# Windowed attention and a squared-ReLU MLP: one list plan for all engines from the second chunk on, second products spread between the seven, weights streamed in seven pieces

## The chip, the core and the metric

The kernel runs on one core of a Trainium2 chip. The metric is the device time of one execution in microseconds (us). Five instruction queues work beside each other, each in its own fixed order: PE (matrix products), DVE and ACT (element-wise work and reading of PSUM, the accumulation banks), POOL (element-wise work on SBUF) and SP (issues nearly all DMA transfers). An instruction waits on semaphores for what it reads, and everything behind it on its own queue waits with it.

## The reference

```python
q, k, v: (8, 8, 576, 64)  w_in: (512, 2048)  w_out: (2048, 512)
scores = q @ k.T / 8 - slope[h] * |i - j|       # keys with 0 <= i - j < 128 only
attn   = softmax(scores)
x      = concat over heads of attn @ v          # (4608, 512)
out    = relu(x @ w_in) ** 2 @ w_out            # (4608, 512)
```

## The kernel before

The 4608 tokens are cut into nine **chunks** of 512, the 2048 hidden units into 16 blocks f of 128. Numbers are split into a high and a low part, so every product takes three matmuls (high by high, high by low, low by high).

In chunks 0 and 1 a block of hidden units is a **first product** of 12 matmuls (line 222); its bank is read by the Relu on ACT (line 232), then squared on DVE and split again into `hh` and `hl`. From chunk 2 on two blocks are made together, as **pair** n = 8c + j, by **the seven** (lines 295 to 345): seven products M1 to M7 of six half-width matmuls each, in the manner of Strassen, on sums of weights and sums of inputs. Three pieces of PSUM hold them: `chain`, through which M1, M6, M7 and M4 accumulate, and two halves of `rest`. Between the products these pieces must be read (**drained**) into `four`: M6 waits until ACT has copied `chain` after M1 (line 315), M2 until DVE has copied `rest` (319), M7 for line 322, M3 and M4 for the additions of line 312. The **second product** of a block f (line 359) is four **parts** of three matmuls, one for each 128 output columns.

The sums of weights are made once, in chunk 1, by `weight_sums` (lines 243 to 271: six additions on POOL, a split on ACT and DVE, per pair j) and kept in DRAM. `stream` (273) brings them back for each pair in two DMA transfers, of 1024 and 768 KB.

Attention runs ahead of the MLP. A **couple** q is one chunk and one pair of heads, in two **segments** s = 0, 1. A **visit** on PE, after every fourth first product and later after every second pair, does three things: it multiplies couple q - 1's probabilities with its values, half of them (line 702), makes couple q's scores (709), and finishes the values. For each segment of couple q then follows its **probability chain**: copy (594, 601) on ACT, masking (613, 617) on DVE, minimum (381) on DVE and exponential (388) on ACT four times, sums (395, 396), scaling (400) on POOL, a block transposition (452) on DVE, four DMA writes of 64 KB to DRAM (456), one read of 256 KB back in another order (461), and two selections on POOL (465). The next visit needs both segments' selections. The values of couple q - 1 are split on ACT, DVE and POOL (`tee`, `tees`, lines 666 to 691); for head pairs p = 2 and 3 they also give the sums of inputs, and with p = 3 the next chunk is complete.

What sets the order: `Plan` (line 793) is a list scheduler; steps have an engine, a duration, predecessors, a due time and rooms (buffers) that they take and free, and it emits step by step what could start first, the earliest due among those. Before, only `start` (847), chunk 0 with the attention ahead of it, is planned by it. From chunk 1 on (lines 991 to 1023) PE's order is as written, and the other engines' order is made by the framework's own scheduler from its timing model, steered by priorities (`high_priority`) and one dependency (`soft`, after the Relu or the first drain).

## Time and profile before

| what | us |
|---|---|
| runs shown: 1006.80, 1003.14, 1007.87; median | 1006.80 |
| profiled execution, its own time | 1004.76 |
| its span, first to last instruction | 1003.1 |
| PE busy | 936.0 |
| DVE / ACT / POOL busy | 602.3 / 435.1 / 290.8 |
| first product of chunk 1 starts | 141.4 |
| first of the seven (chunk 2) starts | 269.2 |
| last chunk's own pairs (no visits) start | 908.9 |

Busy shares are means over stages with different limits; what bounds a stage is read from who waits for whom in it. A busy PE is not PE at its full rate: the granted clock stands in a row of its own.

### The profile page before, as it was taken

The page shows a single profiled execution, that of the slowest core. Times are in us where ns is not written, and L with a number is a line of the kernel's source. Part 1 is how long each engine was busy: PE and PEld are TensorE (multiplying, and loading weights), DVE is VectorE, ACT ScalarE, POOL GpSimd, SP SyncE. Part 2 cuts the span into 40 slices and gives each one's busy share as a digit, 9 for nine tenths or more (in the row PEclk, how much of TensorE's full clock was granted, in tenths as well). Part 3 has the DMA queues.
Part 4 walks back from the last instruction along what each step waited for, and adds up shares of the span by engine and source line. Part 5 has one row for each costly group of instructions (what it writes and reads, how often), then busy time and mean ns, then how long its engine had stood idle before and what let it go on. Part 6 is the DMA issues. An engine that isn't in the chain of part 4 may idle for free.

```text
span 1003.1 us, 22438 instructions
## 1 busy us (share of the span) xinstructions
PE 936.0 (93%) x8496; PEld 817.7 (82%) x8500; DVE 602.3 (60%) x1622; ACT 435.1 (43%) x1241; POOL 290.8 (29%) x362
## 2 busy tenths in 40 slices
PE   9898999978789989999999989999999989999998
PEld 5687887757679878898888878888898878988997
DVE  6987855465545565566666656666565574665333
ACT  7897644344434434334434434343343433443222
POOL 4112335785622222222322232223222322221000
PEclk9999999998989999999999999999999999999999
DMA  9986633457476666676666657767766675555541
GB/s 350 404 315 210 196 82 142 121 189 247 133 264 227 225 205 200 230 231 225 213 218 229 228 180 256 227 226 226 266 225 214 214 224 178 199 183 213 182 147 43
DMA packets 95819, 212.89 MB, mean 212 GB/s; under 512 B 10464, under 2 KB 44384, under 8 KB 88544
## 3 DMA queue, kind: packets, MB, share of 16 engines
q1 hardware_dynamic: 95280, 210.81, 63.2%
q8 instruction: 67, 1.10, 0.4%
q10 hardware_dynamic: 432, 0.66, 0.2%
q14 instruction: 40, 0.33, 0.1%
HBM read 170.52 MB, written 40.89 MB: 211 GB/s over the span
## 4 chain that ended last, share of the span: by engine, by line
PE 52%; DMA 17%; DVE 12%; POOL 8%; ACT 6%; issue 3%; SPq 1%; POOLq 0%; DVEq 0%; ACTq 0%
PE acc L359 22%; PE chain L309 10%; PE rest L309 8%; DMA pp<-way 5%; PE g L222 4%; POOL pp L465 4%; DMA way<-pp 3%; DMA flow<-ws 3%; PE s L702 3%; DVE t L381 3%; DVE t L613 3%; DMA raw<-in_dram 2%; PE g L709 2%; ACT t L601 2%; ACT t L388 2%
## 5 line engine op out<-in xcount | busy, mean ns | idle before, releaser
L359 PE MATMUL acc<-hh,w 128*128 128x512 f32 x1152 | 411.1, 399 | 0.0
L359 PEld LDWEIGHTS acc<-hh,w 128*128 128x128 f32 x1152 | 226.6, 197 | 39.0 <-issue 5.6
L359 PE MATMUL acc<-hl,w 128*128 128x512 f32 x576 | 227.1, 394 | 0.0
L465 POOL TENSOR_SCALAR_AFFINE_SELECT pp<-pp 128x512 f32<-128x512 f32 x128 | 104.0, 820 | 306.3 <-DMA pp<-way 196.0
L309 PEld LDWEIGHTS rest<-xu,flow 128*128 128x128 f32 x1008 | 147.6, 198 | 24.0 <-DVE four L319 10.0
L309 PE MATMUL chain<-tees,flow 128*128 128x256 f32 x1008 | 152.4, 287 | 13.6 <-ACT four L315 12.3
L309 PE MATMUL rest<-xu,flow 128*128 128x256 f32 x1008 | 150.7, 286 | 9.3 <-DVE four L319 5.6
L309 PEld LDWEIGHTS chain<-tees,flow 128*128 128x128 f32 x1008 | 134.7, 199 | 18.1 <-ACT four L315 15.6
L359 PEld LDWEIGHTS acc<-hl,w 128*128 128x128 f32 x576 | 113.2, 197 | 12.0
L312 DVE TENSOR_TENSOR four<-four,rest 128x256 f32<-128x256 f32 x112 | 46.9, 419 | 111.6 <-PE rest L309 111.0
L336 ACT COPY four<-chain 128x256 f32<-128x256 f32 x56 | 20.9, 373 | 211.8 <-PE chain L309 211.8
L388 ACT ACTIVATE t<-t,nm 128x128 f32<-128x128 f32 x256 | 100.4, 394 | 26.0 <-DVE nm L381 25.7
L222 PE MATMUL g<-xu,w 128*128 128x512 f32 x384 | 98.9, 407 | 11.2 <-ACT r L232 11.2
L400 POOL TENSOR_TENSOR t<-t,nm 128x512 f32<-128x512 f32 x64 | 68.0, 1066 | 142.5 <-DVE nm L396 139.5
L222 PEld LDWEIGHTS g<-xu,w 128*128 128x128 f32 x384 | 78.0, 214 | 26.7 <-ACT r L232 13.3
L343 DVE SCALAR_TENSOR_TENSOR four<-four 128x512 f32<-128x512 f32 x112 | 81.7, 766 | 2.5 <-ACT four L336 0.4
L345 DVE TENSOR_TENSOR hl<-four,hh 128x512 fp32r<-128x512 f32 x112 | 77.2, 718 | 6.7
L702 PE MATMUL s<-pp,v 64*64 64x64 f32 (+1 forms) x1792 | 61.1, 261 | 21.1 <-POOL pp L465 21.0
L344 ACT CAST hh<-four 128x512 fp32r<-128x512 f32 x112 | 68.8, 620 | 23.0 <-DVE four L343 22.6
L319 DVE COPY four<-rest 128x256 f32<-128x256 f32 x56 | 23.4, 418 | 87.1 <-PE rest L309 86.8
L702 PEld LDWEIGHTS s<-pp,v 64*64 64x64 f32 x1792 | 46.6, 141 | 33.7 <-POOL pp L465 27.3
L452 DVE STREAM_TRANSPOSE pp<-t 128x512 f32<-128x512 f32 x64 | 44.8, 706 | 34.7 <-POOL t L400 32.7
(102 smaller groups left out, 1102.7 us busy)
## 6 DMA issues: line engine op xcount, KB each, us to landing
flow<-ws SPq DMA_DIRECT2D x56, 1024.0 KB, 5.4
flow<-ws SPq DMA_DIRECT2D x56, 768.0 KB, 5.3
raw<-in_dram SPq DMA_DIRECT2D x32, 512.0 KB, 8.7
way<-pp SPq DMA_DIRECT2D x256, 64.0 KB, 3.2
pp<-way SPq DMA_DIRECT2D x64, 256.0 KB, 3.7
qk<-in_dram SPq DMA_DIRECT2D x32, 320.0 KB, 3.9
v<-in_dram SPq DMA_DIRECT2D x32, 320.0 KB, 4.4
qk<-in_dram SPq DMA_DIRECT2D x38, 256.0 KB, 4.6
```

The source lines that it names most:

```text
L222: nc.tensor.matmul(g, w, xs[cc][:, part], start=i == 0, stop=i == 11)
L309: nc.tensor.matmul(to, w, x, start=start and k == 0, stop=k == 5, skip_group_check=True)
L312: add = lambda to, x: nc.vector.tensor_tensor(to, to, x, op=ALU.add)
L343: nc.vector.scalar_tensor_tensor(r, r, 0.0, r, op0=ALU.max, op1=ALU.mult)
L344: nc.scalar.copy(hh, r)
L345: nc.vector.tensor_tensor(hl, r, hh.bitcast(F32), op=ALU.subtract)
L359: nc.tensor.matmul(self.acc[m], w, h, start=(f == 0 and i == 0), stop=(f == NF - 1 and i == 2))
L388: return self.nc.scalar.activation(self.t[:, m], self.t[:, m], AF.Exp, bias=nm[:, 4 + m : 5 + m], scale=-1.0, accum_out=nm[:, m : m + 1],)
L400: self.nc.gpsimd.tensor_tensor(*(x.rearrange("p (j i) c -> p j i c", j=2) for x in (self.t, self.t)), self.rec.unsqueeze(3).to_broadcast([ ...
L452: nc.vector.transpose(squares.rearrange("p b m c -> p m b c"), self.t.rearrange("p m (b c) -> p m b c", c=32))
L465: nc.gpsimd.affine_select(to, self.own, pattern=[[-32 * sign, 4], [0, 4], [-sign, 32]], compare_op=op, fill=0.0, base=0, channel_multiplie ...
L702: made.append(mm(to, w, x, start=first and n < 2, stop=not first, skip_group_check=True))
```

## The change

From chunk 1 on `middle` lists every step of every engine for a second `Plan`, with durations and due times, and the plan emits them; the framework's scheduler orders nothing any more. PE's order is still as listed, as each PE step has the one before as predecessor. Within it:

- **Second products** lag one part further and stand two by two between the seven: M1, two parts, M5 M6, two, M2 M7, two (one in even pairs), M3 M4, two (three after a visit). Before it was one part in each of the first three gaps and five behind M4.
- **Visits** stand right behind M4 of odd pairs; before one more part lay between.
- **Weights** come in seven transfers of 256 KB into seven rooms; each is issued for pair n + 2 once the product of pair n that read its room is done. For odd pairs they also wait for the plan's step that reads back the probabilities of a certain earlier visit.
- **`weight_sums`** becomes single steps, one pair j behind every second first product; before two pairs j were issued behind each visit. Its ACT and DVE steps and the transfers of its results are halved.
- The squares go to rooms of their own (`r`, `spare`), so that `four` is free earlier; memsets of masked columns become steps of their own (`fill`); copying out (`give`) and sending (`send`) too.
- The values' split becomes eleven (or six) steps. They are due late, but for p = 3, where the next chunk needs them.

```diff
+    def stream(self, n, i):
+        self.nc.sync.dma_start(self.flow[n % 2][i].bitcast(F32), self.sums[n % 8][:, i])
...
+    def squared(self, n, f):
...
+        x, r = self.four[f], self.spare if f else self.hp.tile([128, 512], F32, name="r", bufs=1)
+        nc.vector.scalar_tensor_tensor(r, x, 0.0, x, op0=ALU.max, op1=ALU.mult)
...
-    def __init__(self):
-        self.steps, self.count = {}, {}
+    def __init__(self, wait=WAIT, port=PORT):
+        self.steps, self.count, self.wait, self.port = {}, {}, wait, port
...
+DRAINS = {
+    "s1": (ACT, 0.32, "M1"), "R": (DVE, 0.4, "M5"), "s2": (ACT, 0.32, "M6"), "C11": (DVE, 0.4, "M2"),
+    "C22": (DVE, 0.4, "M7"), "C12": (DVE, 0.4, "M3"), "C21": (ACT, 0.32, "M4"),
+}
+BEHIND = {"M6": ("s1",), "M2": ("R",), "M7": ("s2",), "M3": ("C11",), "M4": ("C22",)}
...
+def middle(K, waiting):
+    P = Plan(0.7, ("t", "ws"))
...
+    def chain(q, s, V):
...
+        d = V + (7.5 if s else 5.5)
+        for m in range(4):
+            P.add(n("t", m), DVE, 0.22, (n("t", m - 1) if m else n("fold"),), V + 1.8 + 1.4 * s, do(G.top, m))
+            P.add(n("e", m), ACT, 0.4, (n("t", m),) + ((n("e", m - 1),) if m else ()), V + 2 + 1.5 * s, do(G.exp, m))
+        P.add(n("sum"), DVE, 0.42, (n("e", 3),), d + 2.2, G.sums)
+        P.add(n("norm"), POOL, 1.15, (n("sum"),), d + 2.7, G.norm)
+        turned(q, s, d + 4, (n("norm"),))
+
+    def turned(q, s, d, after):
...
+        P.add(n("square"), DVE, 0.72, after, d, step, "pp", "t")
+        P.add(n("write"), "SP", 1.8, (n("square"),), d + 1, step)
+        P.add(n("read"), "SP", 1.4, (n("write"),), d + 4.9, step)
+        P.add(n("before"), POOL, 0.81, (n("read"),), d + 8.2, step)
+        P.add(n("same"), POOL, 0.81, (n("before"),), d + 9, step)
...
+    def stream(n, i, t):
+        gate = 2 * ((2 * n - 7 - FIRST) // 4 + 9) + 1
+        if n < FULL:
+            after = [(PIECES[i], n - 2)] if (PIECES[i], n - 2) in P.steps else []
...
+            if n % 2 and ("read", gate) in P.steps:
+                after.append(("read", gate))
+            P.add(("flow", n, i), "SP", 0.8, tuple(after), t + 17, do(K.stream, n, i))
...
+        counts = (2, 2, 2, 3 if n % 2 else 2) if n % 2 or n >= FULL - 8 else (2, 2, 1, 2)
...
+            if names[0] == "M3" and V:
+                visit((2 * n + 1 - FIRST) // 4 + 9)
+            second(count)
```

Three places in the order, before and after. **First, POOL in chunk 1**, ahead of its third visit. `both` are sums of weights, `pp` the probabilities that the visit waits for (line 465 before, 484 now). Before:

```order
L258 TENSOR_TENSOR both4_2523<-w7_606 128x512
L465 AFFINE_SELECT pp_2220<-pp_2220 128x512
L267 TENSOR_TENSOR both2_2230<-both2_2230 128x256
L258 TENSOR_TENSOR both4_2523<-w7_606 128x512
L465 AFFINE_SELECT pp_2220<-pp_2220 128x512
L264 TENSOR_TENSOR both4_2523<-both4_2523 128x256
L465 AFFINE_SELECT pp_2303<-pp_2303 128x512
L266 TENSOR_TENSOR both4_2523<-both4_2523 128x256
L265 TENSOR_TENSOR both4_2523<-both4_2523 128x256
L465 AFFINE_SELECT pp_2303<-pp_2303 128x512
```

POOL after, at the same visit:

```order
L261 TENSOR_TENSOR both4_2038<-w7_606 128x512 x2
L268 TENSOR_TENSOR both4_2038<-both4_2038 128x256
L270 TENSOR_TENSOR both4_2038<-both4_2038 128x256
L484 AFFINE_SELECT pp_2358<-pp_2358 128x512 x2
L484 AFFINE_SELECT pp_2366<-pp_2366 128x512 x2
L272 TENSOR_TENSOR both4_2038<-both4_2038 128x256
L274 TENSOR_TENSOR both4_2038<-both4_2038 128x256
```

The four selections now stand together; before five weight sums lay between them.

**Second, PE and ACT at pair 28**, the first pair behind a visit. On PE `acc` are second products, `chain` and `rest` the seven. PE before:

```order
L309 MATMUL chain_4907<-xu_3513,flow4_1694 128x256 x3
L359 MATMUL acc_4372<-hh_4763,w8_677 128x512
L359 MATMUL acc_4372<-hl_4764,w8_677 128x512
L359 MATMUL acc_4372<-hh_4763,w8_677 128x512
L309 MATMUL rest_4908<-xu_3178,flow4_1694 128x256 x3
L309 MATMUL rest_4908<-xu_3513,flow4_1694 128x256 x3
L309 MATMUL chain_4907<-tees12_1685,flow4_1694 128x256 x6
```

PE after, from the same product M1 to the same product M6:

```order
L319 MATMUL chain_4941<-xu_3639,flow4_0_1673 128x256 x3
L376 MATMUL acc_4473<-hh_4745,w6_576 128x512
L376 MATMUL acc_4473<-hl_4746,w6_576 128x512
L376 MATMUL acc_4473<-hh_4745,w6_576 128x512
L376 MATMUL acc_4438<-hh_4847,w8_677 128x512
L376 MATMUL acc_4438<-hl_4848,w8_677 128x512
L376 MATMUL acc_4438<-hh_4847,w8_677 128x512
L319 MATMUL rest_4967<-xu_3232,flow4_1_1674 128x256 x3
L319 MATMUL rest_4967<-xu_3639,flow4_1_1674 128x256 x3
L319 MATMUL chain_4941<-tees12_1664,flow4_2_1675 128x256 x6
```

Between M1 and M6, which needs the copy of `chain`, there are now two parts and M5, before one part and M5.

ACT there, before (601 and 594 copy the scores, 388 are exponentials, 315 is the copy that M6 waits for, 670, 671 and 674 split the values):

```order
L601 COPY t_4848<-g_4800 128x2x128
L594 COPY t_4846<-g_4800 128x512
L670 CAST xu_4859<-s_4783 128x256
L671 COPY o_4860<-s_4783 128x256
L388 ACTIVATE t_4846,nm_4847<-t_4846,nm_4847 128x128 x4
L315 COPY four_1698<-chain_4907 128x256
L388 ACTIVATE t_4848,nm_4849<-t_4848,nm_4849 128x128 x4
L674 CAST xu_4859<-o_4860 128x256
L322 COPY four_1698<-chain_4907 128x256
```

ACT after (613 and 620, 407, 327 and 331, 684 to 688 in the same roles):

```order
L613 COPY t_4385<-g_4855 128x512
L620 COPY t_4682<-g_4855 64x2x128
L620 COPY t_4682<-g_4855 128x2x128
L407 ACTIVATE t_4385,nm_4386<-t_4385,nm_4386 128x128 x4
L327 COPY four0_1687<-chain_4941 128x256
L407 ACTIVATE t_4682,nm_4683<-t_4682,nm_4683 128x128 x4
L351 CAST hh_4981<-spare_1689 128x512
L686 CAST xu_4987<-s_4827 128x256
L331 COPY four0_1687<-chain_4941 128x256
L684 COPY o_4994<-s_4827 128x256
```

One segment's copy comes first now, and the values' split has moved behind the exponentials.

**Third, SP at the same pair** (`flow` are weights, `way` the probabilities' writes to DRAM, `pp` their reads). Before:

```order
L456 DMA way_4551<-pp_4549 32x4x128 x4
L278 DMA flow4_1694<-ws4_112 128x2048
L461 DMA pp_4549<-way_4551 128x512
L456 DMA way_4600<-pp_4598 32x4x128 x4
L278 DMA flow6_1695<-ws4_112 128x1536
L461 DMA pp_4598<-way_4600 128x512
L278 DMA flow8_1696<-ws5_113 128x2048
```

SP after:

```order
L288 DMA flow4_0_1673<-ws4_112 128x512
L175 DMA v_4631<-in_1_dram 128x640
L288 DMA flow4_1_1674<-ws4_112 128x512
L288 DMA flow4_2_1675<-ws4_112 128x512
L475 DMA way_4669<-pp_4667 32x4x128 x4
L480 DMA pp_4667<-way_4669 128x512
L475 DMA way_4719<-pp_4707 32x4x128 x4
L480 DMA pp_4707<-way_4719 128x512
L288 DMA flow4_3_1676<-ws4_112 128x512
L288 DMA flow4_4_1677<-ws4_112 128x512
```

Nothing but the probabilities' own transfers stands between their first write and their last read now; before two transfers of weights lay there.

More of the change, by code (lines that the diff above doesn't have):

```diff
@@ L625, in begin, with fill @@
         self.base(s)
[L627 to L639 removed]
+    def fill(self, s):
+        self.room(s)
+        self.base(s, True)
     def values(self):
@@ L694, in visit @@
-def visit(K, old, new):
-    nc, mm = K.nc, K.nc.tensor.matmul
-    S = K.sc.tile([128, 2, 512], F32, name="s")
-    def phase(rows, first):
-        made = []
-        for n, pair in enumerate(zip(*(G.quarters(S, r) for G, r in zip(old.both, rows)))):
-            for to, w, x in pair:
-                made.append(mm(to, w, x, start=first and n < 2, stop=not first, skip_group_check=True))
-        return made
-    last = phase((0, 1), True)[-1]
-    if new:
-        new.S, new.B = S, K.big.tile([128, 2, 512], F32, name="g")
-        for extra, to, w, x in new.quarters():
-            made = mm(to, w, x, start=not extra, stop=True, skip_group_check=True)
-            last = made if extra else last
-    turn = nc.gpsimd.nop()
-    K.tc.add_manual_dep(turn.ins, last.ins.name, SYNC, reason="halves of the keys change banks")
-    for made in phase((1, 0), False)[:2]:
-        K.tc.add_manual_dep(made.ins, turn.ins.name, SYNC, reason="halves of the keys change banks")
-    if old.both[0].p == 3:
-        old.out(S)
-    if new:
-        new.front()
-    if old.both[0].p < 3:
-        old.out(S)
-    if new:
-        new.both[0].soft()
+        one, two = slice(0, 256), slice(256, 512)
@@ L843, in run @@
                 do()
+            for a in then.get(name, ()):
+                need[a] -= 1
+                if need[a] == 0:
+                    near.add(a)
+        assert len(end) == len(self.steps), sorted((set(self.steps) - set(end)), key=str)
         return end
```

531 lines of the change are left out of this document (337 added, 194 removed).

## The prediction

> **What bounds the kernel now.** The page first: of all engines PE alone is busy nearly throughout, and its clock digit is 8 in one slice of 40 and 9, the highest, in the others.
>
> ```profile
> PE 936.0 (93%) x8496; PEld 817.7 (82%) x8500; DVE 602.3 (60%) x1622; ACT 435.1 (43%) x1241; POOL 290.8 (29%) x362
> PEclk9999999998989999999999999999999999999999
> ```
>
> The change takes no matmul away, so the question is how far PE's stages are from running without a gap. The view of busy time by stretch, cut at the first product of chunk 1, at the first of the seven and at the last chunk's pairs (columns: stretch, its length, busy us of PE, weight loads, DVE, ACT, POOL, then clock and DMA share):
>
> ```profile
> 141.40:269.20 127.80, 108.77 (x870) 90.74 (x870) 64.38 (x135) 47.65 (x116) 82.08 (x87) 0.95 0.49 159
> 269.20:908.90 639.70, 602.96 (x6071) 540.00 (x6070) 387.88 (x1116) 257.50 (x818) 166.75 (x223) 0.98 0.68 221
> 908.90:1003.10 94.20, 90.42 (x553) 82.26 (x551) 36.85 (x68) 21.12 (x44) 1.29 (x2) 1.00 0.40 140
> ```
>
> What such a stretch takes without gaps stands in the chain that ended last (start, us), at places where PE follows PE:
>
> ```profile
> 149.93 2.76 PE acc L359 x12
> 152.69 2.76 PE g L222 x12
> ...
> 429.17 0.83 PE s L702 x32
> 431.89 3.00 PE acc L359 x12
> 453.35 0.20 PE s L702
> ...
> 947.83 3.49 PE acc L359 x15
> 958.43 3.49 PE acc L359 x15
> ```
>
> A first product takes 2.76 us, a second one 2.76, a pair in the last chunk 958.43 - 947.83 = 10.60. From one visit to the next with nothing in the way it is 453.35 - 429.17 = 24.18, of which the visit is 431.89 - 429.17 = 2.72. So **chunk 1** could take 16 x 5.52 + 4 x 2.72 = 99.2 against 127.8, and the **24 periods** of two pairs and a visit 24 x 24.18 = 580.3 against 639.7. Lost are 28.6 and 59.4, together 88.0 us. The last chunk loses nothing (8 x 10.60 and the 9.1 of the second products left over make 93.9 of its 94.2), and chunk 0 isn't touched.
>
> Who PE waited for in the two stretches (us in total, times, longest), chunk 1 in the first two rows:
>
> ```profile
> PE g L222 <- ACT r L232: 10.5, 4, 3.5
> PE s L702 <- POOL pp L465: 7.3, 2, 5.0
> ...
> PE s L702 <- POOL pp L465: 13.6, 18, 2.5
> PE chain L309 <- ACT four L315: 12.3, 13, 2.7
> PE rest L309 <- DVE four L319: 5.6, 4, 2.9
> ```
>
> Two kinds: a drain or Relu that came late, and a visit that waited for selections. The waits shown are about half of the 88 us; a good part of the rest is the clock after them. One drain wait in the timeline, what ACT did just before (chain), and the stretch behind:
>
> ```profile
> 383.12 1.26 ACT t L388 x6
> 384.38 0.27 ACT four L315
> ...
> 384.69 0.99 PE L309 MATMUL chain<-tees,flow 128*128 128x256 f32 x6 [2.44 <-ACT four L315]
> ...
> 385.70:389.10 3.40, 3.40 (x15) 3.17 (x15) 1.35 (x4) 0.74 (x5) 1.31 (x2) 0.51 0.29 61
> ```
>
> The copy that M6 needs stood behind exponentials; PE was idle for 2.44 us and then ran 3.4 us at a granted 0.51, which costs 1.7 more.
>
> **The change part by part.** *Drains and Relus (chunk 1: 10.5 and its clock; later 12.3 + 5.6 and theirs).* In the order, two parts and M5 (2 x 0.70 + 0.72 = 2.1 us) now cover the copy of `chain` where one part and M5 (1.4) did. The copy itself takes about 0.4, with at most four exponentials of about 0.4 ahead of it, and the values' split has gone behind. What would be late next is the second segment's sums on DVE, with a drain behind them. I take 0.1 per period; the bounds are 0 and today's (12.3 + 5.6) / 24 = 0.75.
>
> *POOL in chunk 1.* Ahead of its third visit the four selections stretched over 226.02 - 216.18 = 9.8 us for 4.1 of their own, with weight sums between:
>
> ```profile
> 216.18 0.96 POOL L465 TENSOR_SCALAR_AFFINE_SELECT pp<-pp 128x512 f32<-128x512 f32 x1 [0.25 <-issue]
> 218.92 0.73 POOL L465 TENSOR_SCALAR_AFFINE_SELECT pp<-pp 128x512 f32<-128x512 f32 x1
> 221.37 1.18 POOL L465 TENSOR_SCALAR_AFFINE_SELECT pp<-pp 128x512 f32<-128x512 f32 x1
> 224.81 1.21 POOL L465 TENSOR_SCALAR_AFFINE_SELECT pp<-pp 128x512 f32<-128x512 f32 x1
> ```
>
> Now they stand together. But POOL's 82.1 us stay, 83% of a stage of 99.2, with a wait for a transfer in each visit, so not all of it can go. I leave 2 us for each of the four visits and 3 for the border to chunk 2, where the seven need sums of inputs that a visit has just made: 11 of 28.6. Bounds: 5 and 28.6. Halving the splits adds eight ACT and eight DVE instructions and 16 transfers; on engines busy for 47.7 and 64.4 of the 127.8 I cost them at nothing, within these bounds.
>
> *Visits from chunk 2 on (13.6 and the clock).* The best case of before, a visit that ends at 856.45 and is followed by one at 878.03 without a wait (chain, SP's and POOL's rows):
>
> ```profile
> 856.45 3.00 PE acc L359 x12
> ...
> 863.59 1.77 SPq L456 DMA_DIRECT2D way<-pp  x4
> 867.14 2.06 SPq L456 DMA_DIRECT2D way<-pp  x4
> 869.37 0.36 SPq L461 DMA_DIRECT2D pp<-way  x1
> 873.15 0.32 SPq L461 DMA_DIRECT2D pp<-way  x1
> ...
> 876.29 1.52 POOL L465 TENSOR_SCALAR_AFFINE_SELECT pp<-pp 128x512 f32<-128x512 f32 x2 [1.09 <-DMA pp<-way]
> ...
> 878.03 0.47 PE s L702 x13
> ```
>
> First write 7.1 after the visit, last selection 21.4 after it; PE leaves 24.18 - 2.72 = 21.5. So even the best visit had no slack, and most of the window goes to transfers. Their medians from issue to landing, in chunk 1 (almost no weights on the way) and later:
>
> ```profile
> way<-pp SPq DMA_DIRECT2D x32, 64.0 KB, 2.0
> pp<-way SPq DMA_DIRECT2D x8, 256.0 KB, 2.8
> ...
> flow<-ws SPq DMA_DIRECT2D x48, 1024.0 KB, 5.5
> way<-pp SPq DMA_DIRECT2D x192, 64.0 KB, 3.7
> pp<-way SPq DMA_DIRECT2D x48, 256.0 KB, 4.1
> ```
>
> The new order has a price: SP stands at the first segment's read until its writes have landed, and the second segment's writes stand behind. From the first write on: 1.35 to the last of four issues (1.77 x 3/4), landing w, read issue 0.35, again 1.35 and w, read r, two selections 1.6, in all 4.65 + 2w + r. The first write comes about 0.5 earlier (one segment's copy, line 594, 0.6, no longer ahead), so 6.6 after the visit. With the medians of chunk 1 the selections end 6.6 + 4.65 + 4.0 + 2.8 = 18.1 after the visit, with the later ones 22.8, against 21.5: no wait, or 1.3. No weights are issued between, but a few pieces lie just ahead; I take 0.4. Every fourth visit (p = 3) makes ACT, DVE and POOL split the values first; there I take 2.0. With the drains' 0.1 per period and two half-clock stretches behind the longest of these waits (1.7 each, from the row above), 18 x 0.4 + 6 x 2.0 + 24 x 0.1 + 3.4 = 25.0 of today's 59.4 remain. Bounds: 5 and 59.4.
>
> *Weights in seven pieces.* 1792 KB per pair as before. They landed 5.5 us after the issue, with two transfers of a pair often on the way together, and a product's room is free two pairs, 21.2 us, before its next use. For odd pairs the reads of a visit, some 4 us later, come first; the cover that is left is 21.2 - 4 - 5.5, about 11 us. Issues on SP take 0.32 to 0.45 each (rows above: 1.77 for four): five more per pair, 2.3 us of 10.6, on a queue that mostly waits. I take 0; bounds 0 and, were all of it in front of the visit's writes, 2.3 per period.
>
> *The clock.* In the row above a gap of 2.44 us led to half clock, so gaps that remain near that length cost 1.7 more. The Trainium skill's "TensorE: Matmul & The Clock Gate", section "Why this matters for your kernels", wants gaps under about 3 us; by that none of my remaining gaps would cost clock, and the sum would be 3.4 us lower. The trace disagrees, with 0.51 behind 2.44 us, and the sum keeps its own.
>
> **Sum:** 1004.8 (the profiled execution, 0.2% under the median of 1006.8, so no correction) - (28.6 - 11) - (59.4 - 25.0) = 1004.8 - 17.6 - 34.4 = 952.8, say **953**.
>
> **Rivals.** *Everything hidden.* Landings as in chunk 1 and drains never late leave the lower bounds, 5 + 5: 1004.8 - 23.6 - 54.4 = 927. For it: 18.1 against 21.5. Against: p = 3 and POOL's 83%.
>
> *The visit takes the place of the drains.* Landings stay at 3.7 and 4.1: 18 x 1.3 + 6 x 3.3 = 43.2, and the six longer gaps cost 1.7 each, 10: 53 of 59.4 remain. 1004.8 - 17.6 - 6.2 = 981. For it: the window was full before; against: the weights no longer lie between.
>
> *It does not do what it says.* The plan's durations are off (its Plan gives a write and its read 3.2 on SP and 2.0 of handing over, where the rows give 1.35 + 3.7 + 4.1), each queue then stands in a wrong order and new waits replace the old ones: within 5 us of 1004.8, say 1003.
>
> *Slower.* The serial order on SP becomes the period: a visit's selections come so late that each period is as long as one of the worst before, from visit to visit:
>
> ```profile
> 479.62 0.78 PE s L702 x24
> ...
> 508.26 1.05 PE s L702 x24
> ```
>
> 28.64, or 4.46 over 24.18. 24 x 4.46 = 107 in place of 59.4: 1004.8 - 17.6 + 47.6 = 1035. It decides from (59.4 + 17.6) / 24 = 3.2 us per period on, which the selections reach (24.7 after the visit) with w and r each 0.6 above the later medians, or with the first write 1.9 late, as a waiting step at the head of DVE's queue can make it.
>
> *Weights in line.* Were a piece to wait for the one before, each would take at least the 2.8 us of a 256 KB read: 7 x 2.8 = 19.6 per pair, 9.0 over 10.6, and 48 x 9.0 = 432 in place of the 59.4 give 1360. Against it: the four writes above were issued within 1.77 us and landed 2.0 to 3.7 after their issue, so they overlapped. The rule that points there is in the Trainium skill, "DMA: Bandwidth & Descriptors", section "Anatomy of one DMA — SWDGE (gpsimd) path": a fixed cost of about 2.0 us per transfer besides its bytes, by which seven pieces one after another would be an estimated 18 us per pair; the rows of overlapping writes decide against reading it so.
>
> **How the numbers follow.** The forecast has 0.60 (940 to 970 by the errors of its terms), everything hidden 0.13, the visit in the drains' place 0.12, not as it says 0.05, slower 0.09, weights in line 0.01. The range 930 to 986 takes in the forecast, the visit rival and the near part of the hidden one and leaves out about 0.2. A measurement of this kernel tells changes over 0.5% from none; faster by more gets 0.60 + 0.13 + 0.12 = 0.85, within 0.05, slower 0.09 + 0.01 = 0.10.
>
> **What would show it.** Drains right: rows of PE waiting for the copies of `chain` and `rest` under 3 us in all. POOL right: waits for selections in chunk 1 under 8 us, the stage near 110. Visits right: reads issued 11 to 13 and 15 to 18 us after a visit, period near 25.2; landings near 4 mean the rival. Weights right: no PE wait for `flow`. Clock right: a mean granted clock of 0.99. Wrong it would be if periods stay over 26.5, if PE waits for `hl` or for values that are split late, or if the first stretch, to 141.4, changes.

## The result, and the profile after

| | us |
|---|---|
| before, median of 4 runs | 1006.75 |
| changed, median of 4 runs (924.34 to 931.54) | 928.09 |
| ratio, with its 95% interval | 0.922 (0.918 to 0.927) |
| predicted | 953, range 930 to 986 |

Faster, as forecast, but 25 us more so, and just below the range; the rival "everything hidden" had said 927. The same kernel in a later session gave 922.64 (0.918, 0.915 to 0.920). The profiled execution took 931.54 us, the slowest of its four.

The page of the changed kernel answers to the two lines shown first of the page of before:

```profile
PE 909.1 (98%) x8500; PEld 804.6 (87%) x8500; DVE 609.9 (66%) x1637; ACT 436.4 (47%) x1249; POOL 289.3 (31%) x355
PEclk9999999999999999999999999999999999999999
```

PE is busy for 98% of a shorter span, and no slice of the clock stands at 8 any more. PE's busy time fell by 26.9 us (936.0 to 909.1) with not one matmul less. Most of that is the clock: the trace of before has eleven stretches of 3.4 us at half clock ahead of its last stage, this one has one, and ten times 1.7 is 17; the other 10 were not traced to a cause. The stretches, cut at the same places as before (stretch, length, busy us of PE, weight loads, DVE, ACT, POOL, clock, DMA share, GB/s):

```profile
139.29:244.20 104.91, 101.84 (x866) 85.78 (x867) 68.28 (x144) 46.29 (x120) 76.67 (x80) 1.00 0.74 240
244.20:834.79 590.59, 583.09 (x6069) 531.99 (x6068) 387.31 (x1119) 259.19 (x821) 166.58 (x221) 1.00 0.76 242
```

Chunk 1 takes 104.9 for 127.8, the 24 periods 590.6 for 639.7 (the last chunk 95.0 for 94.2). Against the 99.2 and 580.3 that they take without a gap they lose 5.7 and 10.3; before it was 28.6 and 59.4. Whom PE still waits for in the whole span (us in total, times, longest):

```profile
PE chain L319 <- POOL tees L669: 2.9, 1, 2.9
PE s L718 <- issue: 2.7, 3, 1.2
...
PE s L718 <- POOL pp L484: 1.3, 2, 1.0
```

The copies of `chain` (ACT) and `rest` (DVE), 17.9 us before, are gone from the list, and selections (POOL pp) went from 21.0 in the whole span to 1.3. Three visits wait another 2.7 for nothing that the profile names (the row with `issue`). The first row is the border to chunk 2, and the one place where the clock still falls:

```profile
254.87 0.58 PE L319 MATMUL chain<-tees,flow 128*128 128x256 f32 x1 [2.88 <-POOL tees L669]
...
254.88:258.28 3.40, 3.40 (x13) 3.11 (x14) 1.30 (x3) 0.00 (x0) 3.18 (x6) 0.52 0.46 99
```

There M7 needs a sum of inputs which POOL makes behind a weight sum and a scaling. One visit in the middle of the run, PE, SP and POOL (start, us):

```profile
584.88 0.90 PE L718 MATMUL s<-pp,v 64*64 64x64 f32 x32
587.60 0.51 PE L376 MATMUL acc<-hh,w 128*128 128x512 f32 x1
609.03 0.90 PE L718 MATMUL s<-pp,v 64*64 64x64 f32 x32
...
594.64 1.76 SPq L475 DMA_DIRECT2D way<-pp  x4
597.81 0.34 SPq L480 DMA_DIRECT2D pp<-way  x1
598.26 1.95 SPq L475 DMA_DIRECT2D way<-pp  x4
601.96 0.34 SPq L480 DMA_DIRECT2D pp<-way  x1
602.35 7.10 SPq L288 DMA_DIRECT2D flow<-ws  x11
...
600.61 1.78 POOL L484 TENSOR_SCALAR_AFFINE_SELECT pp<-pp 128x512 f32<-128x512 f32 x2 [2.91 <-PE chain L319]
604.80 1.52 POOL L484 TENSOR_SCALAR_AFFINE_SELECT pp<-pp 128x512 f32<-128x512 f32 x2 [2.41 <-DMA pp<-way]
```

From visit to visit 609.03 - 584.88 = 24.15, the period without a gap. First write 7.0 after the visit's end (587.6), reads 10.2 and 14.4 after it, last selection at 606.32, 18.7 after; PE leaves 21.4. So 2.7 us of slack stand here where there was none, and all weights go in one go of eleven pieces behind the second read. This visit is among the better ones: over 23 visits from 269 us on, the last selection ends 17.7 to 21.4 us after the visit (once 22.9), half of them by 19.5, while PE leaves 21.4. What the transfers took from issue to landing (270 to 905 us):

```profile
flow<-ws SPq DMA_DIRECT2D x364, 256.0 KB, 4.5
way<-pp SPq DMA_DIRECT2D x184, 64.0 KB, 2.1
pp<-way SPq DMA_DIRECT2D x46, 256.0 KB, 2.8
```

Writes and reads of probabilities land as fast as in chunk 1 before (2.0 and 2.8), not in the 3.7 and 4.1 that they took beside weights.

### The profile page after: what moved, and what is told of

Same layout as the page of the kernel before. It is cut to its first block, busy times and chain, and to the rows that moved or that the text cites. A ratio compares the mean times of both kernels' runs of the same rounds, so it can differ in the third digit from the quotient of the medians.

```text
span 929.8 us, 23237 instructions
## 1 busy us (share of the span) xinstructions
PE 909.1 (98%) x8500; PEld 804.6 (87%) x8500; DVE 609.9 (66%) x1637; ACT 436.4 (47%) x1249; POOL 289.3 (31%) x355
## 4 chain that ended last, share of the span: by engine, by line
PE 87%; DMA 5%; DVE 3%; ACT 2%; issue 1%; POOL 1%; SPq 0%; POOLq 0%; DVEq 0%; ACTq 0%
PE acc L376 41%; PE chain L319 17%; PE rest L319 13%; PE g L224 7%; PE s L718 5%; PE g L731 2%; DMA raw<-in_dram 2%; DMA qk<-in_dram 1%; PE s L731 1%; PE at L496 1%; DVE t L400 1%; DMA wide<-in_dram 1%; DMA ws<-both 1%; POOL pp L484 1%; DVE t L632 0%
## 5 line engine op out<-in xcount | busy, mean ns | idle before, releaser
L376 PE MATMUL acc<-hh,w 128*128 128x512 f32 x1152 | 405.8, 397 | 0.0
L484 POOL TENSOR_SCALAR_AFFINE_SELECT pp<-pp 128x512 f32<-128x512 f32 x128 | 99.4, 778 | 188.0 <-DMA pp<-way 140.1
L419 POOL TENSOR_TENSOR t<-t,nm 128x512 f32<-128x512 f32 x64 | 72.0, 1127 | 219.0 <-ACT t L407 117.0
L339 ACT COPY four<-chain 128x256 f32<-128x256 f32 x56 | 20.9, 373 | 220.9 <-PE chain L319 220.9
L407 ACT ACTIVATE t<-t,nm 128x128 f32<-128x128 f32 x256 | 100.0, 393 | 25.8 <-DVE nm L400 25.0
L224 PE MATMUL g<-xu,w 128*128 128x512 f32 x384 | 95.5, 397 | 2.2 <-DVE xu L662 1.4
L400 DVE CUSTOM_DVE_ANT_0 t<-t,cst 128x128 f32<-128x128 f32 x256 | 67.6, 318 | 1.5
L632 DVE COPY_PREDICATED t<-cst,s 64x256 f32<-64x256 int32 x100 | 44.6, 446 | 34.4 <-PE s L718 24.4
L718 PE MATMUL s<-pp,v 64*64 64x128 f32 (+1 forms) x1792 | 54.2, 248 | 4.3 <-issue 2.7
L669 POOL TENSOR_TENSOR tees<-lows,tees 128x256 fp32r<-128x256 f32 x35 | 28.5, 827 | 82.6 <-ACT tees L704 77.7
L331 ACT COPY four<-chain 128x256 f32<-128x256 f32 x56 | 20.7, 370 | 67.6 <-PE chain L319 67.0
L319 PEld LDWEIGHTS chain<-xu,flow 128*128 128x128 f32 x336 | 48.7, 196 | 4.2
```

The source lines that it names most:

```text
L224: nc.tensor.matmul(g, w, xs[cc][:, part], start=i == 0, stop=i == 11)
L319: self.nc.tensor.matmul(to, w, x, start=start and k == 0, stop=k == 5, skip_group_check=True)
L376: self.nc.tensor.matmul(self.acc[m], w, h, start=(f == 0 and i == 0), stop=(f == NF - 1 and i == 2))
L400: self.nc.vector.tensor_tensor_reduce(self.t[:, m], self.t[:, m], self.K.nrel(2 * self.p + m // 2), -0.125, BIG, ALU.add, ALU.min, self.nm ...
L407: return self.nc.scalar.activation(self.t[:, m], self.t[:, m], AF.Exp, bias=nm[:, 4 + m : 5 + m], scale=-1.0, accum_out=nm[:, m : m + 1],)
L419: self.nc.gpsimd.tensor_tensor(*(x.rearrange("p (j i) c -> p j i c", j=2) for x in (self.t, self.t)), self.rec.unsqueeze(3).to_broadcast([ ...
```

## The experiments

The question is which part made the gain, and why more came than was forecast. For every run, where its time lies, measured in its own trace, one execution: chunk 1 (first product of chunk 1 to the first of the seven), and all chunks with the seven (to the last of `chain`).

| run | median us | ratio to before (95%) | chunk 1 | the seven |
|---|---|---|---|---|
| before | 1006.75 | | 127.8 | 721.0 |
| changed | 928.09 | 0.922 (0.918 to 0.927) | 104.9 | 674.2 |
| f2 | 1020.76 | 1.016 (1.011 to 1.021) | 126.9 | 732.7 |
| f3 | 986.76 | 0.981 (0.978 to 0.985) | 127.4 | 706.1 |
| f4 | 975.74 | 0.969 (0.967 to 0.972) | 126.5 | 693.8 |
| e1 | 1104.29 | 1.099 (1.091 to 1.108) | 110.2 | 836.8 |
| e2 | 928.21 | 0.923 (0.917 to 0.929) | 105.3 | 669.0 |
| e3 | 938.20 | 0.933 (0.927 to 0.939) | 105.8 | 677.2 |
| e4 | 960.76 | 0.955 (0.948 to 0.962) | 138.2 | 665.2 |
| e5 | 920.92 | 0.915 (0.913 to 0.918) | 104.2 | 664.7 |
| e6 | 1004.34 | 0.998 (0.995 to 1.000) | 106.8 | 736.2 |
| e7 | 933.78 | 0.927 (0.925 to 0.928) | 106.3 | 672.9 |
| e8 | 939.02 | 0.932 (0.930 to 0.933) | 104.8 | 680.1 |
| e9 | 927.94 | 0.922 (0.920 to 0.923) | 106.3 | 668.7 |
| e10 | 929.18 | 0.921 (0.917 to 0.926) | 105.1 | 673.2 |
| e11 | 939.79 | 0.932 (0.929 to 0.936) | 104.8 | 681.8 |
| e12 | 1077.55 | 1.072 (1.070 to 1.074) | 137.9 | 786.9 |

### Parts of the change alone, on the kernel before (f2, f3, f4)

f2 draws a second part of the second products between the pieces of the seven:

```diff
-            seconds = K.second(*divmod(2 * n - 2, NF))
+            seconds = chain(K.second(*divmod(2 * n - 2, NF)), K.second(*divmod(2 * n - 1, NF)))
...
                 next(seconds)
+                if k < 2 or n % 2 == 0:
+                    next(seconds)
...
```

> The kernel before, with one edit: two parts of second products in place of one between the pieces of the seven, as the change has them. Theory (drains and visits each lose time of their own): the waits on the copies of chain and rest, 12.3 + 5.6 us, go, and some five of eight half-clock stretches (1.7 each) with them: 980 to 990, with 13 us or more of visit waits left. Rival (the visit's window is the bound, the drains only take up its slack): the visit waits grow by what the drains lose, to 25 or more, and the time stays over 997.

f3 makes the weights' two transfers follow the reads of the last visit in SP's order:

```diff
+            made = self.nc.sync.dma_start(x.bitcast(F32), sums[:, 4 * i : 4 * i + 4 - i])
+            for back in self.backs if n > NF + 1 else ():
+                self.tc.add_manual_dep(made.ins, back.ins.name, ORDER, reason="weights behind the reads")
...
```

> The kernel before, with one edit: the weights' transfers are issued behind both reads of the visit. Theory: probabilities then land in about 2.1 (writes) and 2.8 us (reads) where they took 3.7 and 4.1, the visit waits of 13.6 us go with their half-clock stretches, the drain waits of 18 us stay: 985 to 992. Rival (landings were not what ended last, selections and POOL were): landings fall, visit waits stay over 10 us, time over 998. Second rival (weights now late): PE waits for flow, time over 1005.

f4 has both edits.

> The kernel before with both edits. Theory: the two gains add up, 962 to 975; what is then left to 928 is chunk 1 (23 us), which neither edit touches, and the plan's order on ACT, DVE and POOL. Rival (one cause alone): no faster than the better of the two alone. Third view (only the plan's order as a whole does it): over 985.

PE's waits in f2, then in f4:

```profile
PE s L703 <- POOL pp L466: 36.5, 30, 4.7
...
PE chain L310 <- ACT four L316: 8.1, 11, 1.7
PE rest L310 <- DVE four L320: 4.4, 6, 2.2
```

```profile
PE s L705 <- POOL pp L468: 12.1, 8, 4.4
...
PE chain L312 <- ACT four L318: 8.9, 11, 1.5
PE rest L312 <- DVE four L322: 4.1, 6, 2.3
```

f2: the drains wait 5.4 us less, and the visits 15.5 more (21.0 before): the kernel is 1.6% slower. This is the rival "the visit takes the place of the drains", and with this edit alone it holds. f3 gains 1.9%; its writes land in 1.8 us and its reads in 2.9. f4 gains 3.1%, 31 us of the 79, and the spread that cost 14 us alone is worth 11 beside the other edit. So the spread pays only once the order on SP has made room. From chunk 2 on alone, the visits wait 13.6 us before, 28.2 in f2, 5.9 in f3 and 3.8 in f4, which is what is left in the changed kernel (3.7): these two edits account for the visits' waits. What f4 lacks against the changed kernel is 21.6 us in chunk 1, which neither edit touches, and 19.6 in the seven, where PE still waits 13.6 for copies out of PSUM.

### Where the weights stand on SP (e1, e6, e5, e2)

All four are the changed kernel with other rules for `flow`. e1: as soon as their room is free, without waiting for a read.

```diff
-            if n % 2 and ("read", gate) in P.steps:
-                after.append(("read", gate))
-            P.add(("flow", n, i), "SP", 0.8, tuple(after), t + 17, do(K.stream, n, i))
+            P.add(("flow", n, i), "SP", 0.8, tuple(after), t - 1000, do(K.stream, n, i))
```

> The changed kernel, but the weights' transfers are due at once and don't wait for the read of a visit, so they stand between the probabilities' writes and reads on SP again. Landing theory: writes take over 3 us and reads about 4 again (2.1 and 2.8 in the changed kernel), the selections end 22.8 to 24.5 us after a visit, periods grow from 24.2 to 25.5-27, and the time is 955 to 990. Rival, that the earlier places of copies, exponentials and drains on ACT and DVE alone give the slack: periods stay near 24.2, the time at 925 to 933.

It is 10% slower than before, far outside what was expected. SP's rows of e1:

```profile
573.38 1.75 SPq L475 DMA_DIRECT2D way<-pp  x4
575.22 2.90 SPq L288 DMA_DIRECT2D flow<-ws  x4
...
583.17 0.37 SPq L480 DMA_DIRECT2D pp<-way  x1
584.86 1.04 SPq L288 DMA_DIRECT2D flow<-ws  x2
586.00 0.36 SPq L480 DMA_DIRECT2D pp<-way  x1
```

Two things come together there: writes land in 3.0 and reads in 3.7 us, and weights stand ahead of the reads, some of them waiting for a room that a product of PE must free first (584.86 comes 1.3 us behind the row above it). PE waited 125.0 us for selections. e6 and e5 were made to part the two. e6 puts odd pairs' seven pieces between the two segments' writes, at a time when their rooms are free, both reads behind; its last line also moves the due time of even pairs' pieces:

```diff
-        gate = 2 * ((2 * n - 7 - FIRST) // 4 + 9) + 1
+        gate = 2 * ((2 * n - 3 - FIRST) // 4 + 9)
...
-            if n % 2 and ("read", gate) in P.steps:
-                after.append(("read", gate))
-            P.add(("flow", n, i), "SP", 0.8, tuple(after), t + 17, do(K.stream, n, i))
+            if n % 2 and n >= NF + 3 and n < FULL - 8:
+                after.append(("write", gate))
+            P.add(("flow", n, i), "SP", 0.4, tuple(after), now + 30 - 18 * (n % 2), do(K.stream, n, i))
```

e5 has `("e", gate, 3)`, the first segment's last exponential, in the place of `("write", gate)`, and `t + 17 - 4 * (n % 2)` as the due time, so that the pieces stand just ahead of the first writes.

> As the version with the odd pairs' weights ahead of the writes, but the seven pieces stand on SP between the first segment's writes and the second's, and both reads come behind. Their rooms are free by then, so nothing on SP waits for a room. If landings beside weights were what cost the kernel before its visit waits: writes land in 3 to 4, reads in 3.5 to 4.5, reads are issued 3 us later for the seven issues, selections end 22 to 26 after the visit against a window of 21.4, visit waits 25 to 90 us, time 950 to 1010. If only standing behind a transfer that waits for its room costs much (as in the run with weights early): visit waits under 15 us, time under 940.

> The changed kernel, with the odd pairs' seven weight pieces issued just ahead of the visit's writes, late enough that their rooms are free and nothing stands behind them on SP for long. It parts two costs that the run with weights between writes and reads had together: slower landings, and standing behind transfers that wait for a room. If the standing made that run slow: writes land in 3 to 3.7, selections end 1 to 3 us later than in the changed kernel (20 to 23 after the visit), visit waits 2 to 15 us, time 928 to 945. If slower landings alone made it slow: visit waits near 100 us and over 1000.

SP and PE's waits of e6, then SP of e5:

```profile
575.58 6.54 SPq L288 DMA_DIRECT2D flow<-ws  x5
582.44 1.77 SPq L475 DMA_DIRECT2D way<-pp  x4
584.25 3.29 SPq L288 DMA_DIRECT2D flow<-ws  x7
587.64 1.83 SPq L475 DMA_DIRECT2D way<-pp  x4
589.84 4.81 SPq L480 DMA_DIRECT2D pp<-way  x2
...
PE s L718 <- POOL pp L484: 22.9, 18, 2.0
PE chain L319 <- DMA flow<-ws: 21.3, 9, 3.5
```

```profile
581.59 2.84 SPq L288 DMA_DIRECT2D flow<-ws  x6
587.86 1.82 SPq L475 DMA_DIRECT2D way<-pp  x4
...
592.60 1.58 SPq L480 DMA_DIRECT2D pp<-way  x2
```

e6 has lost the whole gain (0.998, 0.995 to 1.000): writes land in 3.5, reads in 3.3, the seven issues alone hold the second writes up for 3.3 us, visits wait for 22.9, and, not expected, PE waits 21.3 for weights, as those came later too. How much of it is landing, how much SP's own time and how much the later weights stays open; the edit as a whole costs 76 us. In e5 the pieces have had some 3 us before the first write; writes land in 2.4, reads in 2.7, and no visit waits for selections any more: 920.9, where 928 to 945 was expected. So weights do no harm some 3 us ahead of the first write or behind the last read; between the chain's transfers they do. e2 streams the weights in two transfers again, behind the reads as in the change:

```diff
-        self.nc.sync.dma_start(self.flow[n % 2][i].bitcast(F32), self.sums[n % 8][:, i])
+        self.nc.sync.dma_start(self.flow[n % 2][i].bitcast(F32), self.sums[n % 8][:, 4 * i : 4 * i + 4 - i])
...
```

> The changed kernel, but a pair's weights come in two transfers of 1024 and 768 KB again, still behind the reads of a visit. Landing theory: what counts is the place on the queue, not the number of pieces; writes stay near 2, reads near 3, the time at 924 to 934. Rival, that the small pieces themselves make the gain: landings over 3, time over 940.

928.21 against 928.09: the seven pieces are worth nothing by themselves; the place is.

### Drains: cover or precedence (e3, e7, e8)

e3 (the first two lines) leaves one part between the pieces and five at the end, e7 (the last two) takes the copies' precedence, e8 has both edits:

```diff
-        counts = (2, 2, 2, 3 if n % 2 else 2) if n % 2 or n >= FULL - 8 else (2, 2, 1, 2)
...
+        counts = (1, 1, 1, 5)
...
-                            (a, n), engine, us, ((m, n),) + also, t - 1000, steps[a], None,
+                            (a, n), engine, us, ((m, n),) + also, t + 3, steps[a], None,
```

> The changed kernel, but one part of the second products in each of the first three gaps between the seven and five behind M4, as before the change. If the cover of two parts is what removed the drains' waits: 10 to 20 us of waits for the copies of chain and rest, with half-clock stretches, time 940 to 955. Rival, that the drains' earlier places on ACT and DVE are enough: under 3 us of such waits, time 926 to 934.

> The changed kernel with one rule of the plan undone: the copies out of PSUM are due 3 us after their product instead of ahead of everything on ACT and DVE. If the two parts between the pieces are cover enough (the prediction's reason), drain waits stay under 3 us and the time within 922 to 933. If precedence is what hides them: drain waits of 6 to 18 us, some with half clock, 936 to 955.

> As the run before, and one part of second products between the pieces instead of two. One part with precedence took 938. If cover and precedence stand in for each other: drain waits 15 to 30 us, 950 to 975. If one part costs its 10 us for another reason and precedence nothing: 936 to 942.

They cost 10, 6 and 11 us beside 928; e7's 6 is no more than an order of equal steps can move (c1 below). PE's waits for copies in e7, then in e8:

```profile
PE rest L319 <- DVE four L329: 3.4, 4, 1.7
PE chain L319 <- ACT four L327: 2.8, 4, 1.0
```

```profile
PE chain L319 <- ACT four L327: 7.9, 8, 2.2
```

6.2 us in e7, more than the 3 that cover alone was to allow, and 8.5 in e8 with 0.6 in two smaller rows; before it was 17.9. In e3 such waits sum to under 2, so precedence makes up for the second part. Its profiled execution is 6.3 us longer than that of the changed kernel: 2.4 of it lie behind the last of `chain`, where more second products are left over, 0.9 in chunk 1 and 3.0 in the seven, less than the 5.2 by which two executions of the changed kernel differ there (674.2 and 669.0). Without cover and precedence together half to two thirds of the drain waits come back (8.5, and 11.6 in e11 below); the rest went with something else in the plan.

### Chunk 1 (e4, e9, e10)

e4 makes the weight sums of two pairs behind each visit, due ahead of everything; e9 makes them one pair at a time, due at once; e10 takes the Relus' precedence. The edit of e4:

```diff
-        if n % 2:
-            j = (n - NF) // 2
+        for j in range((n - FIRST) // 2, (n - FIRST) // 2 + 2) if (n - FIRST) % 4 == 0 and n >= FIRST else ():
...
-            d = t + 20 if j < 6 else t + 60
+            d = t - 1000
```

In e9 only the last line changes, to `d = t`, and in e10 only the Relu's due time, from `t - 800` to `t + 1.8`.

> The changed kernel, but the sums of weights are listed two pairs at a time behind every visit of chunk 1 and due at once, so ten of them stand ahead of a selection of the third visit. If the place of the selections on POOL made chunk 1's gain: the stage from its first product to the first of the seven grows from 104.9 to 115-125 us with a wait of 5 us or more for selections, time 938 to 950. Rival, that the Relus' and drains' places made it: the stage stays under 108, time 926 to 932.

> The changed kernel with the weight sums of chunk 1 due as soon as their pair's first product is done, in place of 20 to 60 us later, pair by pair. The prediction left 11 us lost in chunk 1 where 5.7 were measured; two pairs' sums in one go at once cost 33. If the selections' place ahead of the sums makes chunk 1's gain: the stage takes 110 to 122 instead of 105, visit waits 4 to 15, time 932 to 948. If only bursts of two pairs' sums hurt: the stage stays under 108 and the time under 932.

> The changed kernel with chunk 1's Relus due 1.8 us after their product instead of ahead of everything on ACT. Before the change PE waited 10.5 us for late Relus in chunk 1, with half clock behind some. If the Relus' precedence made chunk 1's gain: waits of 5 to 15 us for r, the stage 112 to 125, time 934 to 948. If the plan puts them well without it: stage under 108, time under 932.

In e4 POOL's rows of a visit show twelve sums ahead of the selections, 14 us of them:

```profile
183.83 2.48 POOL L261 TENSOR_TENSOR both<-w 128x512 f32<-128x512 f32 x2
...
196.99 0.85 POOL L274 TENSOR_TENSOR both<-both 128x256 f32<-128x256 f32 x1
197.80 3.74 POOL L484 TENSOR_SCALAR_AFFINE_SELECT pp<-pp 128x512 f32<-128x512 f32 x4
```

Chunk 1 then takes 138.2, longer than before. But with one pair's six sums ahead of the four selections (e9, 6.6 us of them) it takes 106.3 and with the Relus in turn (e10) 105.1. So neither rule made chunk 1's gain: selections behind one pair's sums cost next to nothing, and behind two pairs' sums that are due ahead of everything they cost 33 us. Which of these two parts of e4 does it, the burst or the precedence of its steps on ACT and DVE as well, was not parted.

### The plan itself (e11, e12)

e11 undoes the four rules together: one part, copies and Relus in turn, sums at once.

> The changed kernel with four rules undone together: copies and Relus due in turn, weight sums due at once, one part of second products between the pieces. What stays is a plan by durations for every engine, with the reads ahead of the weights. If these rules stand in for each other and make the rest of the gain together: 955 to 980, near the 976 of the kernel before with its two edits. If the plan by durations makes it: 936 to 948, the sum of the single runs.

939.8, 12 us over the changed kernel: what the rules are worth together in time is what the cover was worth alone. PE waits 11.6 us for copies (10.2 for `chain`, 1.4 for `rest`). What is left is still 36 us faster than f4, so most of what f4 lacks is in the rest of the change, the plan by durations, the single steps and the squares' own rooms among it. Of these only the durations were taken out in a run of their own. e12 keeps all rules and due times and lets the planner reckon with a quarter of the durations on ACT, DVE and POOL:

```diff
     def add(self, name, engine, us, after, due, do, take=None, free=None):
...
+        if self.wait == 0.7 and engine in (ACT, DVE, POOL):
+            us = us / 4
...
```

> The changed kernel, but the planner reckons every step of ACT, DVE and POOL from chunk 1 on at a quarter of its duration (PE's and SP's stay); the due times, the rules and the work stay, only the order of steps moves. If the durations on those engines are what puts each step in time: waits for copies and selections return, 945 to 985. If the due times, counted from PE's own place, carry the order and the durations hardly matter: 922 to 936. If the time reaches the 976 of the kernel before with its two edits or more, the plan's durations are the whole rest of the gain.

1077.6, 7% slower than before, though the reads still stand ahead of the weights (writes land in 1.8, reads in 3.0). PE's waits of e12:

```profile
PE chain L319 <- ACT four L327: 60.9, 26, 3.5
```

and ACT's rows of a visit, first in e12, then in the changed kernel (L407 exponentials, L327 the copy after M1):

```profile
569.87 0.41 ACT L407 ACTIVATE t<-t,nm 128x128 f32<-128x128 f32 x1 [0.27 <-DVE nm L400]
...
573.82 0.40 ACT L688 CAST xu<-o 128x256 fp32r<-128x256 f32 x1
574.13 0.37 ACT L327 COPY four<-chain 128x256 f32<-128x256 f32 x1
```

```profile
589.16 0.40 ACT L407 ACTIVATE t<-t,nm 128x128 f32<-128x128 f32 x1 [0.79 <-DVE nm L400]
...
590.33 0.39 ACT L407 ACTIVATE t<-t,nm 128x128 f32<-128x128 f32 x1
...
590.84 0.37 ACT L327 COPY four<-chain 128x256 f32<-128x256 f32 x1
591.11 0.40 ACT L407 ACTIVATE t<-t,nm 128x128 f32<-128x128 f32 x1
```

With true durations four exponentials stand ahead of the copy and four behind, so that it comes as M1 ends; a planner that takes exponentials for short puts all eight and three steps of the values ahead of it, and the copy's precedence does not help, since for the plan they were done. With the rules kept, it is the durations that decide whether copies and Relus (14.1 us of waits) come in time; for selections PE waits 0.6, and 10.7 before three visits for another step of POOL (line 735). That shows that the plan needs right durations, not that they alone removed the waits of before: the framework's scheduler had a timing model too, and no run gives it the plan's durations.

### How far a time of this kernel can be trusted (a_again, c1, c2)

Steps that are equal for the planner come in an order that depends on the kernel's text. c1 is the changed kernel, c2 is e5, each with one comment line more; the changed kernel ran beside them.

> The changed kernel once more, beside the next three on one chip: 925 to 932.

> The changed kernel with one comment line more. Steps that are equal for the planner are taken in an order that depends on the text, so some rows on SP, ACT, DVE and POOL change places, by no rule of the plan. If the gain is the rules' own, the time stays within 0.7% of the changed kernel's, 922 to 935, and the one half-clock stretch at the border to chunk 2 may come or go (some 5 us). If it hangs on a lucky order, over 940.

> The version with the odd pairs' weights just ahead of the writes (921 in the job before), with one comment line more. If that version is better by its rule, 918 to 925, and below the changed kernel in this job by over 0.4%. If it was the order of equal steps, it lies within the two times of the changed kernel's texts.

922.64 (ratio 0.915 to 0.920), 930.28 (0.924 to 0.928) and 924.21 (0.917 to 0.921). Equal steps in another order are worth 0.8%. The gain does not hang on them, but differences under 1% between the versions above are not shown to be their rules'. That holds for e5, the fastest: its two texts have 920.9 and 924.2, the change has 922.6, 928.1 and 930.3. It beats the kernel before; that it beats the change is not shown.

## Why the prediction was wrong in size

The gains lie in the stages where they were forecast, the sum was too cautious, and the reason given for the drains did not hold. Term by term, in the profiled execution: chunk 1 lost 5.7 instead of 11 (5.3 less), the periods 10.3 instead of 25.0 (14.7 less), the start took 2.1 less and the last chunk 0.8 more: 952.8 - 5.3 - 14.7 - 2.1 + 0.8 = 931.5. The border to chunk 2, 3 of the 11, lies behind the cut: its waits of 2.9 and 0.7 and its half clock (1.7) stand in the periods' 10.3. Counted where the forecast had it, chunk 1 with the border lost 11.0, as forecast, partly by luck (5.7 for 8 and 5.3 for 3), and the periods 5.0 instead of 25.0: the error of the sum is there.

- **Visits, the step that failed.** "With the medians of chunk 1 the selections end 18.1 after the visit, with the later ones 22.8 ... I take 0.4", and 2.0 for each visit with p = 3, 19.2 in all. The formula came close (median 19.5 over the visits, against 18.1), and the landings were those of chunk 1 throughout. That no weights are issued between was said in the forecast itself. Its reason for more than nothing, a few pieces just ahead, did not slow them: in the visit shown above three pieces are issued up to 0.7 us ahead of the first write, and over all visits writes land in 2.1 and reads in 2.8. Nor did p = 3 cost 2.0 each: there the first write comes 10.0 to 10.4 after the visit, and the selections still end at 20.2 to 21.4 in four of the five that the trace has from 269 us on (22.9 in the other). Measured are 3.7 us of waits in four visits. f3 and f4 show the cause apart from the rest: weights behind the reads bring landings to 1.8 and 2.9, and with the spread beside it the visits' waits to 3.8.
- **Drains.** 0.1 per period forecast, none measured; the list's bound of under 3 us held. But the reason given, two parts of cover, is neither enough nor needed: f2 has two parts and waits 12.5 us, e3 has one and waits 1.6, so that the number held by something else. Precedence of the copies is part of it (6.2 without, e7) and the plan's durations are needed (e12); what removed the rest is argued, not shown.
- **POOL in chunk 1.** Sized at 11, measured 5.7, and the stage took 105, not 110. That selections now stand together was true and not decisive (e9). That POOL is busy for 73% of the stage does not make it late (0.3 us of waits for selections there, but 25.8 with e4's order). What made the 23 us of chunk 1 stays open, beyond that wrong durations lose it (137.9 in e12).
- **Weights in seven pieces** at nothing: right, and with two transfers the same (e2). The Trainium skill's "DMA: Bandwidth & Descriptors", section "Anatomy of one DMA — SWDGE (gpsimd) path", gives a fixed cost of about 2.0 us per transfer for those that gpsimd issues. These are issued by SP, and here five transfers more per pair changed no time that can be measured, as they overlap.
- **Clock.** Two half-clock stretches forecast, one left, mean clock 0.998 (0.99 forecast). It came behind a gap of 2.88 us, as the forecast took it. By the Trainium skill's rule of about 3 us ("TensorE: Matmul & The Clock Gate", section "Why this matters for your kernels") that gap is a borderline case; here it led to 0.52.
- **The rivals.** "Everything hidden", given 0.13, is the one that came: landings as in chunk 1, no late drain, 927 for 928. The visit in the drains' place is what the spread alone does (f2). A plan whose durations are off was given 5% and 1003; with a quarter of the true ones it is 1078 (e12), so its price was far too low. The slower rival, selections late by the order on SP, was priced at 1035; weights ahead of the reads cost 1004 (e6) and 1104 (e1).
- **The start** was to stay at 141.4 and ends at 139.3. Versions of the changed kernel end it at 137.7 to 142.9, those of before at 141.4 to 144.0; why was not tried.

## What to carry to other kernels

When an edit makes a transfer stand alone that was slowed by others, take the landing that the trace shows where it did stand alone, not a value between. Ask first which of two full windows ends last: the spread of second products lost 14 us by itself and gained 11 once the order on SP had made room. An order planned by durations needs right ones: the same rules with a quarter of the true ones lost more than the change had gained.

## What was not expected of the hardware

The length of the gap ahead does not decide by itself whether half clock follows. At the same place, the first product of chunk 1 behind the same wait of 1.41 us, e3 fell to 0.51 and the changed kernel did not (wait in e3, then the stretch in e3, then in the changed kernel):

```profile
139.35 2.17 PE L224 MATMUL g<-xu,w 128*128 128x512 f32 x5 [1.41 <-DVE xu L662]
...
140.00:143.40 3.40, 3.40 (x9) 2.69 (x9) 1.56 (x3) 0.00 (x0) 3.40 (x6) 0.51 0.18 38
```

```profile
139.30:142.70 3.40, 3.40 (x14) 3.08 (x15) 1.60 (x3) 0.16 (x1) 2.71 (x5) 1.00 0.29 61
```

The clock's own rows tell them apart. In each trace the half-clock stretches begin on one grid of 3.41 us (all 24 of e1 are whole steps apart), and the grid lies differently from execution to execution. In e3 the whole wait falls into one cell of it, 136.63 to 140.05, of which PE is busy for 0.51, and the next cell runs at half clock. In the changed kernel a border at 138.65 parts the same wait, and PE is busy for 0.77 and 0.81 of the two cells. Over all 20 traces (from 40 us on), the 99 cells at full clock that half clock follows have PE busy for at most 0.51 of them, the other 5139 for at least 0.44. So in these runs a cell that is idle for about half or more costs another 1.7 us, and a wait of 1.4 to 3 us does so or not by where it falls; two executions of one kernel differ by that. The Trainium skill's "TensorE: Matmul & The Clock Gate", section "Why this matters for your kernels", wants gaps under about 3 us; in these runs that is not enough.

The cost of a queue that stands: in e1 the two reads were issued 16.5 and 19.3 us after a visit (medians), in the changed kernel 11.3 and 15.1, though the first write came no later (6.8 against 7.2). Slower landings of its writes (0.9 us) cannot make these 4 to 5 us; the rest is weights ahead of the reads, by their issues and their waits for rooms. Which of the two had the larger part was not parted.
